# GpSimd's block-by-block weight copies, later output weights and a ScalarE read-out in a convolution and gated feed-forward kernel

## The chip, the core and the metric

The kernel runs on one core of a Trainium2 chip. The metric is the device time in microseconds of one execution; lower is better. Three runs of the kernel before took 766.85, 766.41 and 765.5 us, with a median of 766.41 us. A profiled execution of the same kernel took 766.03 us; its trace covers a span of 764.2 us of that.

The core's engines work side by side, each through its own list of instructions in order: TensorE (PE for its matmuls, PEld for the loads of its stationary operand), VectorE (DVE), ScalarE (ACT), GpSimd (POOL) and SyncE (SP), which here only issues DMA requests. They wait for one another through semaphores.

## The reference

The input x has 8 sequences of 4096 tokens with 192 values. First comes a causal convolution with 7 taps, whose taps are a softmax over the rows of `weight`, one row for each of 8 heads of 24 channels. Its output goes through a gated feed-forward layer.

```python
w = softmax(weight)                      # [8 heads, 7 taps]
x_pad = concatenate([zeros(6 tokens), x])
c[t, h, :] = sum_k w[h, k] * x_pad[t + k, h, :]
gate = maximum(c @ w_gate, 0)            # 192 -> 1536
val  = c @ w_val                         # 192 -> 1536
out  = (gate * val) @ w_out              # 1536 -> 192
```

Activations and weights are float16 in the kernel, sums are float32, and the output is float32.

## The kernel before

**Units and blocks.** Tokens are worked on in 16 units (`NUNIT`). A unit holds 1024 tokens of each of two sequences, called streams: one lies on partitions 0 to 63, the other on 64 to 127. The 192 channels are three chunks `c` of 64. For each unit `gate_val` (line 526) runs twice, once for each window `w` of 512 tokens. A run goes through 12 blocks `f` of 128 hidden columns. A block does six matmuls with `Wg` (three chunks, two streams) and six with `Wv` (line 539), into two PSUM tiles; ScalarE applies the ReLU to the first (line 550) and VectorE multiplies with the second into `hT` (line 551). So block `f` of the first window needs columns 128f to 128f+127 of `Wg` and `Wv`, on both halves of the partitions. After both windows `project` (line 634) multiplies `hT` with `Wo` (line 568), and the results are copied out of PSUM and stored.

**PSUM.** There are four tiles of two banks, used in turn, so a block's tile is free again when its reader of two blocks earlier has finished.

**Where the convolved tokens come from.** For unit 0 the convolution itself runs on TensorE as products with banded matrices (`conv_dense`, line 344). `first_block` (line 371) does the first window before anything else: one PSUM tile for each chunk, copied to `xc[0]` by ScalarE for chunks 0 and 1 and by VectorE for chunk 2 (line 379). `second_block` does the second window in front of block 5 (line 530). From unit 1 on, ScalarE, VectorE and GpSimd convolve from a transposed copy of x, the "lane". `lane_load(v)` (line 187) requests x for unit v into `x_e`, in two pieces with two streams each. `lane_turn(v)` (line 456) is a generator: for each piece GpSimd copies both streams from `x_e` into `x_p` (line 463), then SyncE requests DMA transposes of its tiles into `x_r` (line 467), and then it yields. `load_x(2)` requests a last group of tokens for TensorE's convolution, for the part of unit 1 that the lane does not cover; the steps "x" and "y" of the first projection use it.

**The weights at the start.** `load_w(s)` (line 158) requests slice `s` of `Wg` and of `Wv` from GpSimd's queue, for partitions 0 to 63 alone. The slices are cut at columns 0, 128, 384, 640, 896, 1152 and 1536: slice 0 is block 0, slice 1 blocks 1 and 2, slice 2 blocks 3 and 4, slice 3 blocks 5 and 6, slice 4 blocks 7 and 8, slice 5 blocks 9 to 11. The other half of the partitions is then filled by copies. VectorE makes those of slices 0 (in `first_block`) and 1 (line 692). GpSimd makes those of slices 2 to 5: `pool_halves` copies a slice of `Wg`, then of `Wv`, with one instruction each, and `pool_parts` (slice 2) splits that of `Wv` by blocks.

**The order on GpSimd's queue.** Requests and copies are worked off in the order in which the code names them; a request waits for GpSimd to reach it. After the requests of slices 0 to 2 come two of `load_x(1)`, those of slice 3, the copies of slice 2, the requests of slice 4, `Wg`'s of slice 5, the copies of slice 3, and `Wv`'s request of slice 5 (lines 217 to 226). Lines 694 to 702 go on: the copies of slice 4, the request of `Wo`, the copies of slice 5, the four requests of `lane_load(1)`, the copy of the taps to the upper partitions, two requests of `load_x(2)`, four small memsets in the band tiles, and `lane_turn(1)` with its four copies.

Of the kernel before, what the change touches and what calls it, by code (L numbers as in the profile page):

```python
# [16 lines left out]
def kernel(  # L17
# [12 lines left out]
    nc = tc.nc  # L30
# [7 lines left out]
    NCH = D // 64  # L38
    NBLK = D // 32
    NFF = DFF // 128  # L40
    WIN = 512
# [48 lines left out]
    def load_rest(steps):  # L90
        for _ in steps:
            pass
# [11 lines left out]
    def stage(p0, rows, st, n_st, jj, n):  # L104
        at = room[p0 : p0 + rows, 0, 0, 0:1]
        dims = [[D * GSUB, n_st], [D, n], [1, D]]
        return bass.AP(
            tensor=at.tensor,
            offset=at.offset + D * (GSUB * st + jj),
            ap=[at.ap[0]] + [d for d in dims if d[1] > 1],  # L110
        )
# [3 lines left out]
    def body(st):  # L115
# [11 lines left out]
        out=xts[0][PAD : PAD + FIRST, 0, :, :],  # L127
        in_=bass.AP(
            tensor=x.tensor, offset=x.offset, ap=[[D, FIRST], [NB * S * D, 2], [1, D]]
        ),  # L130
# [22 lines left out]
    Wg = const.tile([128, NCH, DFF], F16)  # L153
    Wv = const.tile([128, NCH, DFF], F16)
    Wo = const.tile([128, NFF, D], F16)
    CUTS = [0, 128, 384, 640, 896, 1152, DFF]

    def load_w(s, which=3):
        cols = slice(CUTS[s], CUTS[s + 1])
        for src, dst in ((moe_w_gate, Wg), (moe_w_val, Wv))[which == 2 : 1 + (which > 1)]:  # L160
            nc.gpsimd.dma_start(
                out=dst[0:64, :, cols],
                in_=src.rearrange("(c p) f -> p c f", p=64)[:, :, cols],
            )

    def both_halves(copy, s, dst):
        cols = slice(CUTS[s], CUTS[s + 1])
        copy(out=dst[64:128, :, cols], in_=dst[0:64, :, cols])

    def pool_halves(s):  # L170
        both_halves(nc.gpsimd.tensor_copy, s, Wg)
        both_halves(nc.gpsimd.tensor_copy, s, Wv)

    def pool_parts(s):
        both_halves(nc.gpsimd.tensor_copy, s, Wg)
        for f0 in range(CUTS[s], CUTS[s + 1], 128):
            nc.gpsimd.tensor_copy(out=Wv[64:128, :, f0 : f0 + 128], in_=Wv[0:64, :, f0 : f0 + 128])  # L177

    xes, xrs, accs, prods = {}, {}, {}, {}

    def pieces(v):
        both = [(0, TDVE, v * UNIT)]
        if v + 1 < NUNIT:
            both.append((TDVE, TILES - TDVE, (v + 1) * UNIT + LDVE))
        return both

    def lane_load(v, hold=None):


        xe = epool.tile([128, TILES, 2, NCH, 64], F16, name="x_e")  # L190
        xes[v] = xe
        for j0, n, t in pieces(v):
            bp, t0 = t // S, t % S
            start = int(t0 == 0)
            if start:
                nc.gpsimd.memset(xe[0:HALO, j0, :, :, :], 0.0)
            for st in range(2):
                b = bp + NB * st
                first = nc.gpsimd.dma_start(  # L199
                    out=xe[:, j0 + start : j0 + n, st, :, :].rearrange("p j c r -> p j (c r)"),  # L200
                    in_=bass.AP(
                        tensor=x.tensor,
                        offset=x.offset + (b * S + t0 - HALO + 128 * start) * D,
                        ap=[[D, 128], [128 * D, n - start], [1, D]],
                    ),
                )
                if hold is not None:
                    tc.add_manual_dep(first.ins, hold.ins.name, SYNC, reason="behind the turns of the lane before")
                    hold = None
                if start:  # L210
                    nc.gpsimd.dma_start(
                        out=xe[HALO:128, j0, st, :, :].rearrange("p c r -> p (c r)"),
                        in_=x[b, 0 : 128 - HALO, :],
                    )
                yield
# [3 lines left out]
    load_w(2)  # L219
    load_rest(load_x(1))  # L220
    load_w(3)
    pool_parts(2)
    load_w(4)
    load_w(5, 1)
    pool_halves(3)
    load_w(5, 2)

    ex = const.tile([H, KW + 1], FP)
    nc.vector.memset(ex[:, KW : KW + 1], 1e-9)
# [21 lines left out]
    with nc.allow_low_precision("zero and one"):  # L251
        nc.vector.tensor_tensor(
            out=same[:], in0=col[:, 0:SEG], in1=s_of[:].to_broadcast([SUB, SEG]), op=ALU.is_equal
        )
        nc.vector.tensor_scalar(
            out=places[:, SUB - SEG : SUB - SEG + NROW],
# [7 lines left out]
        out=mx[:], in_=wr[:], axis=mybir.AxisListType.X, op=ALU.max, negate=True  # L264
# [6 lines left out]
    with nc.allow_low_precision("rounded as the band is"):  # L271
        nc.vector.tensor_scalar(
            out=soft[:],
# [7 lines left out]
        out=spread[0:SUB, 0, 0:H],  # L281
# [7 lines left out]
    with nc.allow_low_precision("products with one and zero"):  # L289
        nc.vector.tensor_tensor(  # L290
            out=diag[:],
# [6 lines left out]
    for a in range(2):  # L298
        for b in range(NSEG):
            nc.tensor.matmul(  # L300
                out=(bps, spread)[a][:, a, HB * SEG * b : HB * SEG * (b + 1)],
# [9 lines left out]
    for cols in (slice(0, 64), slice(64, D)):  # L311
        nc.scalar.copy(
            out=xts[0][0:ROWS0, 1:GSUB, 0, cols],
            in_=stage(0, ROWS0, 0, 1, 1, GSUB - 1)[:, :, cols],
# [25 lines left out]
    xc = {}  # L340
# [30 lines left out]
    def first_block():  # L371
        xc[0] = xcpool.tile([128, NCH, UNIT], F16, name="xc")
        both_halves(nc.vector.tensor_copy, 0, Wg)
        both_halves(nc.vector.tensor_copy, 0, Wv)
        for c in range(NCH):
            ps = psum.tile([128, 2, 512], FP, name="ps")
            conv_dense(0, c, ps, 0)
            copy = nc.vector.tensor_copy if c == 2 else nc.scalar.copy
            copy(out=xc[0][:, c, 0:WIN], in_=ps[:, 0, :])

    def second_block():
        two, one = [psum.tile([128, 2, 512], FP, name="ps") for _ in range(2)]
        conv_dense(1, 0, two, 0)
        conv_dense(1, 1, two, 1)
        nc.scalar.copy(out=xc[0][:, 0:2, WIN : 2 * WIN], in_=two[:])
        conv_dense(1, 2, one, 0)
        nc.vector.tensor_copy(out=xc[0][:, 2, WIN : 2 * WIN], in_=one[:, 0, :])
# [68 lines left out]
    def lane_turn(v):  # L456
        xe = xes.pop(v)
        xp = epool.tile([128, TILES, NCH, 2, 64], F16, name="x_p")
        xr = rpool.tile([128, NCH, 128 * TILES], F16, name="x_r")
        xrs[v] = xr  # L460
        for j0, n, _ in pieces(v):
            for st in range(2):
                nc.gpsimd.tensor_copy(  # L463
                    out=xp[:, j0 : j0 + n, :, st, :], in_=xe[:, j0 : j0 + n, st, :, :]
                )
            for j in range(j0, j0 + n):
                nc.sync.dma_start_transpose(
                    out=xr[:, :, 128 * j : 128 * j + 128],
                    in_=xp[:, j].rearrange("p c s r -> p (c s r)"),
                )  # L470
            yield
# [54 lines left out]
    def gate_val(u, w):  # L526
        h = hpool.tile([128, NFF, 2, WIN], F16, name="hT")
        xcb = xc[u]
        for f in range(NFF):
            if u == 0 and w == 0 and f == 5:  # L530
                second_block()
            pss = [psum.tile([128, 2, 512], FP, name="ps") for _ in range(2)]
            order = [(i, c) for i in range(2) for c in range(NCH)]
            if u == 0 and w == 0 and f == 0:
                order = [(i, c) for c in range(NCH) for i in range(2)]
            for i, c in order:
                W = (Wg, Wv)[i]
                for st in range(2):
                    nc.tensor.matmul(  # L539
                        out=pss[i][:, st, :],  # L540
                        lhsT=W[64 * st : 64 * st + 64, c, 128 * f : 128 * (f + 1)],
                        rhs=xcb[64 * st : 64 * st + 64, c, WIN * w : WIN * (w + 1)],
                        start=(c == 0),
                        stop=(c == NCH - 1),
                        tile_position=(64 * st, 0),
                    )
            by_stream = u == 0 and w == 0 and f < 2
            for sts in (slice(0, 1), slice(1, 2)) if by_stream else (slice(0, 2),):
                gr = gpool.tile([128, 2, WIN], F16, name="gr")
                nc.scalar.activation(out=gr[:, sts], in_=pss[0][:, sts], func=ACTF.Relu)  # L550
                nc.vector.tensor_tensor(  # L551
                    out=h[:, f, sts], in0=gr[:, sts], in1=pss[1][:, sts], op=ALU.mult
                )
        return h
# [127 lines left out]
    for h in range(H):  # L682
        r = G * h
        while r < G * (h + 1):
            c, n = r // 64, min(64 - r % 64, G * (h + 1) - r)
            nc.sync.dma_start(
                out=tap[r % 64 : r % 64 + n, c, :],
                in_=taps[h : h + 1, :].unsqueeze(1).to_broadcast([1, n, KW]),
# [2 lines left out]

    both_halves(nc.vector.tensor_copy, 1, Wg)
    both_halves(nc.vector.tensor_copy, 1, Wv)
    pool_halves(4)
    nc.gpsimd.dma_start(out=Wo[:], in_=moe_w_out.rearrange("(c p) d -> p c d", p=128))
    pool_halves(5)
    load_rest(lane_load(1))
    nc.gpsimd.tensor_copy(out=tap[64:128], in_=tap[0:64])
    load_rest(load_x(2))
    for end in ends:  # L700
        nc.gpsimd.memset(end, 0.0)
    load_rest(lane_turn(1))
    for u in range(NUNIT):
        adds = 1 <= u < NUNIT - 1
        if u + 1 < NUNIT:
# [63 lines left out]
```

## Time and profile before

| | |
|---|---|
| median of 3 runs | 766.41 us (765.5 to 766.85) |
| the profiled execution's own time | 766.03 us |
| its span | 764.2 us |
| HBM read, written | 31.48 MB, 25.17 MB |
| DMA packets of GpSimd's queue (q0) | 41104, 20.6% of 16 engines' span |
| DMA packets of SyncE's and ScalarE's queue (q1) | 90472, 23.3% |

The profile page gives for each engine the time in which it was busy, a chain of waits followed back from the last instruction, and groups of instructions by line with the engine's idle time ahead of them. A row of the timeline reads: start in us from the span's begin, duration, engine, line, operation, output tile and input tiles, shape, count, and in brackets the idle time of the engine ahead of it with what ended that. "POOL L161 DMA_DIRECT2D" is the time in which GpSimd makes a request; the transfer itself goes on behind it. A row of the DMA view gives for requests of one kind their count, the size, and the median time from the start of the request to the landing of its data; a row without a last number has a landing that could not be told. The rows of the queues give packets, megabytes and the share of 16 DMA engines in the view's window.

### The profile page before, as it was taken

What the parts mean: (1) busy time and instruction counts of PE and PEld (TensorE: products, weight loads), DVE (VectorE), ACT (ScalarE), POOL (GpSimd) and SP (SyncE); (2) the same over time, 40 slices, a digit from 0 to 9 for tenths busy, and PEclk for the clock granted to TensorE, in tenths of its full rate; (3) what the DMA queues carried; (4) which work ended last, traced back from release to release, by engine and by line L of the source; (5) the groups of instructions that cost most, each with busy time, mean ns of one, the idle gap of its engine ahead of it and who ended that gap; (6) DMA issues with size and microseconds to landing.
All of it is one profiled execution on the core that took longest, in us unless ns stands there. A gap on an engine that the chain in (4) does not pass through costs nothing.

```text
span 764.2 us, 25118 instructions
## 1 busy us (share of the span) xinstructions
PE 760.4 (99%) x10935; PEld 518.6 (68%) x10935; DVE 705.7 (92%) x768; ACT 600.3 (79%) x733; POOL 378.8 (50%) x249
## 2 busy tenths in 40 slices
PE   9999999999999999999999999999999999999998
PEld 4495775957659576585866858567595775957658
DVE  7998999999999999999999999999999999999891
ACT  6787887878878787887878878787887887876571
POOL 8519448093571916629175390853909347090000
PEclk9999999999999999999999999999999999999999
DMA  9969037280442805529162281832818034220202
GB/s 117 130 111 145 7 97 79 65 114 22 95 64 84 95 24 109 46 85 95 32 113 36 85 94 44 107 29 90 88 44 130 8 98 60 64 49 16 70 1 84
DMA packets 131830, 55.93 MB, mean 73 GB/s; under 512 B 96584, under 2 KB 131720, under 8 KB 131720
## 3 DMA queue, kind: packets, MB, share of 16 engines
q1 hardware_dynamic: 90472, 38.66, 23.3%
q0 software_dynamic: 41104, 15.57, 20.6%
q8 instruction: 85, 1.39, 0.8%
q14 instruction: 25, 0.20, 0.1%
q10 hardware_dynamic: 144, 0.10, 0.0%
HBM read 31.48 MB, written 25.17 MB: 74 GB/s over the span
## 4 chain that ended last, share of the span: by engine, by line
PE 99%; ACT 0%; issue 0%
PE ps L539 65%; PE ps L568 32%; PE ps L617 1%; PE ps L145 0%; PE ps L361 0%; PE ps L300 0%; PE ps L402 0%; ACT acc L594 0%; PE ps L280 0%
## 5 line engine op out<-in xcount | busy, mean ns | idle before, releaser
L551 DVE TENSOR_TENSOR hT<-gr,ps 128x1024 f16<-128x1024 f16 (+1 forms) x386 | 469.1, 1216 | 36.2 <-ACT gr L550 9.4
L550 ACT ACTIVATE gr<-ps 128x1024 f16<-128x1024 f32 (+1 forms) x386 | 393.3, 1020 | 102.5 <-PE ps L539 100.6
L489 POOL TENSOR_TENSOR prods<-prods 128x1344 f32<-128x1344 f32 x70 | 212.3, 3032 | 289.8 <-DVE prods L485 286.4
L539 PE MATMUL ps<-xc,Wv 64*128 64x512 f16 x2304 | 316.6, 376 | 0.0
L539 PE MATMUL ps<-xc,Wg 64*128 64x512 f16 x2304 | 316.2, 376 | 0.0
L568 PE MATMUL ps<-Wo,hT 64*128 64x192 f16 x5952 | 248.8, 243 | 0.0
L568 PEld LDWEIGHTS <-hT 64*128 64x128 f16 x5952 | 246.4, 94 | 3.5
L539 PEld LDWEIGHTS <-Wv 64*128 64x128 f16 x2304 | 136.0, 94 | 113.4 <-POOL Wv L177 0.4
L539 PEld LDWEIGHTS <-Wg 64*128 64x128 f16 x2304 | 123.7, 94 | 121.4 <-issue 0.4
L513 DVE SCALAR_TENSOR_TENSOR acc<-x_r,tap,acc 128x576 f32<-128x576 f16 x225 | 165.3, 811 | 0.0
L483 ACT ACTIVATE prods<-x_r,tap 128x448 f32<-128x448 f16 x222 | 130.0, 660 | 0.0
L594 ACT COPY out_s<-ps 128x768 f32<-128x768 f32 (+1 forms) x64 | 45.6, 713 | 51.2 <-PE ps L568 39.8
L199 POOL DMA_DIRECT2D x_e<-in_x_dram x58 | 47.0, 822 | 15.3 <-ACT acc L499 11.5
L463 POOL COPY x_p<-x_e 128x960 f16<-128x960 f16 (+1 forms) x58 | 50.3, 907 | 0.7 <-DMA x_e<-in_x_dram 0.7
L489 POOL TENSOR_TENSOR xc<-prods 128x1344 f16<-128x1344 f32 x14 | 42.4, 3030 | 1.1
L513 DVE SCALAR_TENSOR_TENSOR xc<-x_r,tap,acc 128x576 f16<-128x576 f16 x45 | 34.1, 811 | 0.0
L499 ACT ACTIVATE acc<-x_r,tap 128x576 f32<-128x576 f16 x45 | 31.4, 763 | 0.0
L485 DVE TENSOR_SCALAR prods<-x_r,tap 128x448 f32<-128x448 f16 x70 | 26.6, 448 | 0.0
L594 DVE COPY out_s<-ps 128x384 f32<-128x384 f32 (+1 forms) x16 | 8.6, 540 | 11.5 <-PE ps L617 9.4
L617 PE MATMUL ps<-Wo,hT 128*128 128x192 f16 x96 | 8.1, 246 | 0.0
L617 PEld LDWEIGHTS <-hT 128*128 128x128 f16 x96 | 7.9, 98 | 0.2 <-issue 0.2
L145 PE MATMUL ps<-const-bfloat16-1.0 128*128 128x512 bf16 (+1 forms) x8 | 3.8, 609 | 0.8 <-PEq L753 0.8
(56 smaller groups left out, 55.9 us busy)
## 6 DMA issues: line engine op xcount, KB each, us to landing
out_dram<-out_s SPq DMA_DIRECT2D x62, 384.0 KB, 2.7
x_e<-in_x_dram POOLq DMA_DIRECT2D x34, 192.0 KB, 7.5
x_e<-in_x_dram POOLq DMA_DIRECT2D x24, 240.0 KB, 5.0
x_r<-x_p SPq DMA_TRANSPOSE x131, 4.7
Wo<-in_moe_w_out_dram POOLq DMA_DIRECT2D x1, 576.0 KB, 6.6
x_h<-in_x_dram POOLq DMA_DIRECT2D x2, 210.0 KB, 6.1
Wg<-in_moe_w_gate_dram POOLq DMA_DIRECT2D x4, 96.0 KB, 4.8
Wv<-in_moe_w_val_dram POOLq DMA_DIRECT2D x4, 96.0 KB, 5.8
```

Of the source, the lines that this page charges most:

```text
L199: first = nc.gpsimd.dma_start(out=xe[:, j0 + start : j0 + n, st, :, :].rearrange("p j c r -> p j (c r)"), in_=bass.AP(tensor=x.tensor, off ...
L463: nc.gpsimd.tensor_copy(out=xp[:, j0 : j0 + n, :, st, :], in_=xe[:, j0 : j0 + n, st, :, :])
L483: engine.activation(out=out, in_=in_, func=ACTF.Copy, scale=scale)
L485: engine.tensor_scalar(out=out, in0=in_, scalar1=scale, scalar2=None, op0=ALU.mult)
L489: nc.gpsimd.tensor_tensor(out=pr[:, 0] if k < KW - 1 else xc[v + 1][:, :, LDVE:UNIT], in0=pr[:, 0], in1=pr[:, k], op=ALU.add,)
L499: nc.scalar.activation(out=accs[v][:, c, :], in_=shifted(v, c, 0, 0), func=ACTF.Copy, scale=tap[:, c, 0:1],)
L513: nc.vector.scalar_tensor_tensor(out=xc[v][:, c, 0:LDVE] if k == KW - 1 else acc[:, c, :], in0=shifted(v, c, k, 0), scalar=tap[:, c, k : k ...
L539: nc.tensor.matmul(out=pss[i][:, st, :], lhsT=W[64 * st : 64 * st + 64, c, 128 * f : 128 * (f + 1)], rhs=xcb[64 * st : 64 * st + 64, c, WI ...
L550: nc.scalar.activation(out=gr[:, sts], in_=pss[0][:, sts], func=ACTF.Relu)
L551: nc.vector.tensor_tensor(out=h[:, f, sts], in0=gr[:, sts], in1=pss[1][:, sts], op=ALU.mult)
L568: mm = nc.tensor.matmul(out=outs[q], lhsT=h[64 * r : 64 * r + 64, f, st, 128 * q : 128 * (q + 1)], rhs=Wo[64 * r : 64 * r + 64, f, :], sta ...
L594: one(out=dst[:, step * j : step * j + step], in_=src[:, step * j : step * j + step])
```

## The change

GpSimd's copies of slices 3, 4 and 5 are made block by block, `Wg` and `Wv` in turn, by `pool_blocks`; each becomes an instruction with 128 columns in three chunks, where it had 256 or 384. Both requests of slice 5 stand together behind the copies of blocks 5 and 6. The requests of `lane_load(1)` come right behind the copies of block 11, then the first half of `lane_turn(1)`, and only then the request of `Wo`. The tap copy, `load_x(2)` and the memsets follow as before, and the second half of `lane_turn(1)` stands at the end. Slice 2 is copied as before (the same three instructions, written out in place). ScalarE now reads out all three chunks of the first convolution. In the very first block TensorE does both first chunks of `Wg`, then both of `Wv`, then the third of each, where it took the chunks in turn.

```diff
-    def load_w(s, which=3):
+    def load_w(s):
         cols = slice(CUTS[s], CUTS[s + 1])
-        for src, dst in ((moe_w_gate, Wg), (moe_w_val, Wv))[which == 2 : 1 + (which > 1)]:
+        for src, dst in ((moe_w_gate, Wg), (moe_w_val, Wv)):
...
-    def pool_halves(s):
-        both_halves(nc.gpsimd.tensor_copy, s, Wg)
-        both_halves(nc.gpsimd.tensor_copy, s, Wv)
-
-    def pool_parts(s):
-        both_halves(nc.gpsimd.tensor_copy, s, Wg)
-        for f0 in range(CUTS[s], CUTS[s + 1], 128):
-            nc.gpsimd.tensor_copy(out=Wv[64:128, :, f0 : f0 + 128], in_=Wv[0:64, :, f0 : f0 + 128])
+    def pool_blocks(*blocks):
+        for f in blocks:
+            cols = slice(128 * f, 128 * f + 128)
+            for dst in (Wg, Wv):
+                nc.gpsimd.tensor_copy(out=dst[64:128, :, cols], in_=dst[0:64, :, cols])
...
     load_w(2)
     load_rest(load_x(1))
     load_w(3)
-    pool_parts(2)
+    both_halves(nc.gpsimd.tensor_copy, 2, Wg)
+    for f in (3, 4):
+        cols = slice(128 * f, 128 * f + 128)
+        nc.gpsimd.tensor_copy(out=Wv[64:128, :, cols], in_=Wv[0:64, :, cols])
     load_w(4)
-    load_w(5, 1)
-    pool_halves(3)
-    load_w(5, 2)
+    pool_blocks(5, 6)
+    load_w(5)
...
             conv_dense(0, c, ps, 0)
-            copy = nc.vector.tensor_copy if c == 2 else nc.scalar.copy
-            copy(out=xc[0][:, c, 0:WIN], in_=ps[:, 0, :])
+            nc.scalar.copy(out=xc[0][:, c, 0:WIN], in_=ps[:, 0, :])
...
             if u == 0 and w == 0 and f == 0:
-                order = [(i, c) for c in range(NCH) for i in range(2)]
+                order = [(0, 0), (0, 1), (1, 0), (1, 1), (0, 2), (1, 2)]
...
     both_halves(nc.vector.tensor_copy, 1, Wg)
     both_halves(nc.vector.tensor_copy, 1, Wv)
-    pool_halves(4)
+    pool_blocks(7, 8, 9, 10, 11)
+    load_rest(lane_load(1))
+    turns = lane_turn(1)
+    next(turns)
     nc.gpsimd.dma_start(out=Wo[:], in_=moe_w_out.rearrange("(c p) d -> p c d", p=128))
-    pool_halves(5)
-    load_rest(lane_load(1))
     nc.gpsimd.tensor_copy(out=tap[64:128], in_=tap[0:64])
     load_rest(load_x(2))
     for end in ends:
         nc.gpsimd.memset(end, 0.0)
-    load_rest(lane_turn(1))
+    load_rest(turns)
```

## The prediction

> **What bounds the kernel now.** I read the page first, for the engine that the end hangs on.
>
> ```profile
> span 764.2 us, 25118 instructions
> PE 760.4 (99%) x10935; PEld 518.6 (68%) x10935; DVE 705.7 (92%) x768; ACT 600.3 (79%) x733; POOL 378.8 (50%) x249
> ...
> PE 99%; ACT 0%; issue 0%
> ```
>
> TensorE fills the span and nearly the whole chain of waits. A change that takes no matmul away can only pay where TensorE stands still, and the edits touch work of the first 50 us. So the second view is TensorE's timeline there (start, length, engine, line, operation).
>
> ```profile
> 7.16 0.39 PE L539 MATMUL ps<-xc,Wg 64*128 64x512 f16 x2
> ...
> 8.33 0.39 PE L539 MATMUL ps<-xc,Wg 64*128 64x512 f16 x2
> ...
> 8.76 0.84 PE L539 MATMUL ps<-xc,Wg 64*128 64x512 f16 x6
> ...
> 11.39 0.81 PE L539 MATMUL ps<-xc,Wg 64*128 64x512 f16 x6
> ...
> 12.88 1.02 PE L539 MATMUL ps<-xc,Wg 64*128 64x512 f16 x6
> ...
> 14.48 1.55 PE L361 MATMUL ps<-band,x_h 110*32 110x104 f16 x120
> 15.96 0.82 PE L539 MATMUL ps<-xc,Wg 64*128 64x512 f16 x6
> ...
> 21.16 0.81 PE L539 MATMUL ps<-xc,Wg 64*128 64x512 f16 x6
> 21.80 0.81 PE L539 MATMUL ps<-xc,Wv 64*128 64x512 f16 x6
> ```
>
> Blocks 5 and 9 begin at 15.96 and 21.16, so a block takes 5.20/4 = 1.30 us and each half of it 0.65: TensorE's own pace. Blocks 0 to 4, from 7.16 to the second convolution at 14.48, take 7.32 us where five blocks at that pace are 6.50. All standing still in the head is thus 0.82 us, and no repair of the head can gain more.
>
> The last place in it where TensorE waits is block 3, which begins at 11.39 and should give way to block 4 at 12.69 but does at 12.88. Two rows name the reason, and the DMA view gives the landing.
>
> ```profile
> 6.06 0.63 POOL L161 DMA_DIRECT2D Wv<-in_moe_w_val_dram  x1
> ...
> 11.88 0.95 POOL L177 COPY Wv<-Wv 64x384 f16<-64x384 f16 x2 [1.45 <-DMA Wv<-in_moe_w_val_dram]
> ...
> 12.43 0.33 PEld L539 LDWEIGHTS <-Wv 64*128 64x128 f16 x5 [0.36 <-POOL Wv L177]
> ...
> Wv<-in_moe_w_val_dram POOLq DMA_DIRECT2D x1, 96.0 KB, 5.8
> ```
>
> Slice 2 of Wv is requested at 6.06, lands 5.8 us later at 11.86, GpSimd copies it from 11.88, and TensorE goes on at 12.43. From there to the second convolution and beyond, every start keeps its pace. So block 3's Wv is a gate: what TensorE gains ahead of it is lost there, unless the gate itself moves.
>
> **The change part by part.** *ScalarE's read-out and the new order in block 0.*
>
> ```profile
> 6.36 1.07 ACT L379 CAST xc<-ps 128x512 f16<-128x512 f32 x2 [0.65 <-PE ps L361]
> ...
> 7.11 0.45 DVE L168 COPY Wv<-Wv 64x384 f16<-64x384 f16 x1 [0.27 <-DMA Wv<-in_moe_w_val_dram]
> ...
> 7.59 0.69 DVE L379 CAST xc<-ps 128x512 f16<-128x512 f32 x1
> ```
>
> VectorE begins chunk 2 only when its Wv copy is over (7.56), ends at 8.28, and TensorE takes chunk 2 at 8.33. ScalarE's two copies fill 1.07, with starts 0.48 apart, so a third runs from about 7.33 to 7.92 and chunk 2 is ready 0.36 us earlier. The new order needs chunk 1 (7.43) second and Wv third, which lands and is copied by 7.56. At 0.216 for a pair of matmuls (0.65/3): first chunk 7.16, Wg's second 7.49, Wv's two 7.70 and 7.92, the third chunk 8.14 and 8.35, block 1 at 8.57. That is 0.19 us ahead of the 8.76 of now. VectorE, rid of 0.69 us, must still wait for slice 1 to land, which I bound between 7.56 and its present copy at 8.31; either way it is not later than now. On the taps' side ScalarE is 0.5 us later, and with it ten small requests on SyncE's queue whose data are needed only at 40 us.
>
> All of this lies ahead of the gate. The requests up to slice 3 and the copies of slice 2 stay in their order on GpSimd's queue, and nothing that VectorE gives up delays them. I take Wv's landing at 11.86 again: the 0.19 us turn into a longer wait at block 3. **0.0 us**; if the gate opened early enough, at most 0.19 (lead) + 0.19 (the gate's own loss) = −0.38.
>
> *Copies by block.* The costs come from GpSimd's timeline.
>
> ```profile
> 8.93 0.64 POOL L161 DMA_DIRECT2D Wv<-in_moe_w_val_dram  x1
> ...
> 14.65 0.84 POOL L168 COPY Wg<-Wg 64x768 f16<-64x768 f16 x1
> ...
> 16.18 0.63 POOL L161 DMA_DIRECT2D Wv<-in_moe_w_val_dram  x1
> ...
> 18.34 1.08 POOL L695 DMA_DIRECT2D Wo<-in_moe_w_out_dram  x1
> 19.42 1.16 POOL L168 COPY Wg<-Wg 64x1152 f16<-64x1152 f16 x1
> ...
> 21.60 3.22 POOL L199 DMA_DIRECT2D x_e<-in_x_dram  x4
> ...
> 26.66 1.90 POOL L463 COPY x_p<-x_e 128x960 f16<-128x960 f16 x2
> ...
> Wv<-in_moe_w_val_dram POOLq DMA_DIRECT2D x1, 96.0 KB, 5.7
> Wg<-in_moe_w_gate_dram POOLq DMA_DIRECT2D x1, 144.0 KB, 3.8
> Wv<-in_moe_w_val_dram POOLq DMA_DIRECT2D x1, 144.0 KB, 3.0
> ```
>
> Starts are 0.45 apart for a copy of one block (two fill 0.95, with an overlap of 0.05), (16.18−14.65)/2 = 0.765 for two blocks, (21.60−19.42)/2 = 1.09 for three. An instruction so costs about 0.14 us beside 0.315 a block. Slices 3 and 4 gain two instructions each and slice 5 four: 8 × 0.14 = 1.1 us more on GpSimd. The Wo request that leaves this stretch takes 1.08 away. The two cancel, and what counts is each block's deadline.
>
> Slice 3's Wv lands at 8.93+5.7 = 14.63. Block 5's Wg copy runs by then; 5 Wv, 6 Wg, 6 Wv start at 14.65, 15.10, 15.55, and the requests of slice 5 at 16.0 and 16.63. Blocks 7 and 8 start at 17.26, 17.71, 18.16, 18.61. Slice 5 lands after 3.0 to 3.8 us: Wg between 19.0 and 19.8, Wv between 19.6 and 20.4. So block 9's copies end by 20.3 and 20.9, and TensorE takes them at 21.16 and 21.80: 0.9 us to spare, where now the slice's Wv copy ends at 21.66, 0.14 ahead. Blocks 10 and 11 follow at 0.45 a copy against TensorE's 0.65. **0.0 us**; bounds below. A gain is excluded here, as no row of TensorE after 12.43 names a weight copy.
>
> *x first, Wo behind it.* The last copy starts 2.25 us after block 9's Wg at the earliest (19.06) and 1.8 after its Wv at the latest (20.4), so the x_e requests begin between 21.8 and 22.65 (now 21.60). The rest of the chain:
>
> ```profile
> 28.59 13.05 SPq L467 DMA_TRANSPOSE x_r<-x_p  x9
> ...
> 40.58 2.14 PE L568 MATMUL ps<-Wo,hT 64*128 64x192 f16 x48
> ...
> 43.06 2.89 ACT L483 ACTIVATE prods<-x_r,tap 128x448 f32<-128x448 f16 x5
> ...
> 47.22 0.80 ACT L594 COPY out_s<-ps 128x768 f32<-128x768 f32 x1 [0.54 <-PE ps L568]
> ...
> x_e<-in_x_dram POOLq DMA_DIRECT2D x2, 240.0 KB, 4.8
> Wo<-in_moe_w_out_dram POOLq DMA_DIRECT2D x1, 576.0 KB, 6.6
> x_r<-x_p SPq DMA_TRANSPOSE x2, 2.5
> ```
>
> GpSimd now waits for x_e ahead of Wo, and behind that wait stand Wo, the tap copy, two x_h requests, the memsets and the second piece. The second stream's request begins 0.87 after the first and lands 4.8 later, at 27.5 to 28.3; its copy takes 0.95, so Wo is requested at 28.4 to 29.3 and lands 6.6 later, at 35.0 to 35.9. TensorE takes it at 40.58: 4.7 us to spare. The two x_h, a third of Wo's bytes each, are requested by 31.2 and, even at Wo's 6.6, land by 37; TensorE takes them after the first half projection, at 42.7. The second piece's copies end by 34.1, and SyncE reaches its transposes only after five others (5/9 of 13.05 us from 28.4 on: 35.7), so they are not late by it. The nine transposes as a whole shift by −0.2 to +0.7. The last lands now at 28.59+13.05−1.26+2.5 = 42.9, and ScalarE's products that read it start at 43.06, so these can start up to 0.5 late. ScalarE has 0.54 us idle ahead of 47.22, and the bank that this copy frees is wanted after 40.58 + four half projections of 2.15, beyond 49. **0.0 us**.
>
> The sum is 0.0 against the profiled execution's 766.03 us. Its runs gave a median of 766.41, 0.38 higher, so I put the time at 766.3.
>
> **The rivals.** *Wo comes late (slower).* It decides when Wo lands after 40.58. For it: Wo's request now sits behind a wait for x, and its transfer meets the transposes of 28.59 to 41.64, which the old one, over by 24.9, did not. If sharing doubles Wo's 6.6 us to 13.2 from 29.3 on, it lands at 42.5, TensorE stands 1.9 us: 768.3. Against it: it must take 11.3 us, and the two kinds already overlapped for the last x_e and x_h. The Trainium skill (DMA: Bandwidth & Descriptors, section SWDGE vs HWDGE vs iDMA) says that requests of GpSimd and of SyncE feed different queues inside a DMA engine, which serves them in turn; by that the doubling would be the worst case, and no row of this trace shows Wo beside transposes.
>
> *Block 9 waits.* Slice 5's Wv is requested at 16.63 instead of 16.18. At the 5.8 us of the slowest row it lands at 22.4, its copy ends at 22.95, and TensorE stands 1.2 us at 21.80: 767.6. Against it: that row came from the crowded first 12 us; both rows of slice 5 are under 4.
>
> *The gate opens earlier.* A queue's row bears on it, of the stretch from 8.2 to 10.5 us.
>
> ```profile
> q8 instruction: 1, 0.02, 5.8%
> ```
>
> One packet of instructions took 5.8% of 16 engines over 2.3 us, which is 2.1 us of one engine, just while Wv's slice 2 was on its way. If it is what made 5.8 us of that landing, a shift of it against Wv would open the gate: −0.38, or 766.0; with every stall of the head gone −0.82, or 765.6. The Trainium skill (Runtime: NRT & Kernel Launch, section Instruction fetch mechanics) says that an engine's instructions come by DMA in blocks of 16 KiB, asked for by its own sequencer as it runs; the packet's 0.02 MB agrees. Against the rival: the first convolution, before which nothing changes, has brought TensorE through its first 240 instructions already, and the requests before slice 3 keep their times.
>
> *The change doesn't do what it says* can be left out for the copies; for the read-out it is the gate again.
>
> **How the numbers follow.** About 0.2% (1.53 us) is what a measurement of this kernel can tell from no change. No net effect beyond 0.4 us: 0.75. Gate opening: 0.10, within 0.2% since its most is 0.82. Block 9: 0.06, also within it. Wo late: 0.05, slower. Left over, 0.02 each for faster and slower by something not seen. So faster 0.02, same 0.91, slower 0.07. The single runs spread from 765.5 to 766.85; the range goes from 765.2 (the gate's 0.38 and half of that spread, 0.7) to 767.6 (block 9's price).
>
> **What would show it.** Right: ScalarE's row of line 379 counts three, TensorE's block 1 starts near 8.57, the weight load of block 3's Wv still waits for GpSimd to about 12.43, block 4 starts near 12.88 and the convolution at 14.48; Wo's first matmul at 40.6, with its request near 29. Wrong: a gap in TensorE's rows at block 9 or ahead of Wo's first matmul, or Wv's copy of slice 2 starting clearly before 11.8.

## The result, and the profile after

The changed kernel takes 768.13 us (median of 17 runs, 767.32 to 770.86) against 766.07 for the kernel before (17 runs, 765.5 to 769.6): 2.06 us more, a ratio of 1.0026 with a 95% interval of [1.0017, 1.0035]. The forecast was no difference, with a range that ended at 767.6.

The profiled execution of the changed kernel took 767.42 us, 1.39 more than the one of before; its span is 1.1 us longer. From its page, the head line and the chain of waits:

```profile
span 765.3 us, 25127 instructions
...
PE 97%; DMA 2%; POOL 0%; issue 0%; ACT 0%; POOLq 0%
```

The chain was all TensorE before. Now 2% of it is a DMA, and the line below it in the page gives x_h as its target. Where time is lost is read from TensorE's own starts. The head first (timeline, columns as before):

```profile
8.59 0.86 PE L537 MATMUL ps<-xc,Wg 64*128 64x512 f16 x6
...
12.52 0.81 PE L537 MATMUL ps<-xc,Wg 64*128 64x512 f16 x6
...
13.91 1.59 PE L360 MATMUL ps<-band,x_h 110*32 110x104 f16 x120
15.43 0.82 PE L537 MATMUL ps<-xc,Wg 64*128 64x512 f16 x6
```

Block 1 starts at 8.59 as worked out (8.57). Block 4 starts at 12.52 and block 5 at 15.43, where they started at 12.88 and 15.96: in this execution the gate at block 3 opened early, and TensorE was 0.53 us ahead. Then the first projection and unit 1:

```profile
10.90 0.96 POOL L222 COPY Wv<-Wv 64x384 f16<-64x384 f16 x2 [0.46 <-DMA Wv<-in_moe_w_val_dram]
...
22.01 3.26 POOL L196 DMA_DIRECT2D x_e<-in_x_dram  x4
...
28.60 0.98 POOL L461 COPY x_p<-x_e 128x960 f16<-128x960 f16 x1 [1.48 <-DMA x_e<-in_x_dram]
29.53 1.03 POOL L696 DMA_DIRECT2D Wo<-in_moe_w_out_dram  x1
...
40.45 2.15 PE L566 MATMUL ps<-Wo,hT 64*128 64x192 f16 x48 [0.21 <-DMA Wo<-in_moe_w_out_dram]
43.50 0.34 PE L400 MATMUL ps<-x_h,band 64*128 64x192 f16 x4 [0.90 <-DMA x_h<-in_x_dram]
...
43.78 2.11 ACT L497 ACTIVATE acc<-x_r,tap 128x576 f32<-128x576 f16 x3 [3.13 <-DMA x_r<-x_p]
...
59.32 0.84 PE L537 MATMUL ps<-xc,Wg 64*128 64x512 f16 x6
...
60.14 0.82 PE L537 MATMUL ps<-xc,Wv 64*128 64x512 f16 x6
```

- Wo's first matmul should come at 40.58 − 0.53 = 40.05 and comes at 40.45: 0.40 lost.
- The half projection ahead of x_h's matmuls took 40.58 to 42.56 before, so these should start at 42.43. They start at 43.50: 1.07 lost.
- In unit 1 the second Wv group starts 0.82 after its Wg group instead of 0.65. The profile names no releaser for it. VectorE's last read-out of the projection ends at 60.09, 0.05 ahead of that start, so I read it as a wait for VectorE, whose sums had begun 2.69 us late behind ScalarE's first sum (line 497), which waited 3.13 us for the transposed x: 0.17 lost.

So −0.53 + 0.40 + 1.07 + 0.17 = 1.1, the span's difference. From there to the end TensorE's starts keep this distance. The DMA view of the requests of 29 to 36 us shows the cause next to hand; its last row is of the kernel before, for the transposes requested from 28 to 34 us:

```profile
Wo<-in_moe_w_out_dram POOLq DMA_DIRECT2D x1, 576.0 KB, 10.9
x_h<-in_x_dram POOLq DMA_DIRECT2D x2, 192.0 KB, 11.9
x_r<-x_p SPq DMA_TRANSPOSE x4, 7.4
...
x_r<-x_p SPq DMA_TRANSPOSE x4, 4.1
```

Wo lands after 10.9 us (6.6 before), x_h after 11.9, and the first transposes after 7.4 (4.1 before). Those requested from 37 to 41 us land after 6.2, where the last ones of before took 2.5.

### The profile page after: what moved, and what is told of

It reads as the page before. It is cut to its first block, busy times and chain, and to the rows that moved or that the text cites. A ratio compares the mean times of both kernels' runs of the same rounds, so it can differ in the third digit from the quotient of the medians.

```text
span 765.3 us, 25127 instructions
## 1 busy us (share of the span) xinstructions
PE 760.0 (99%) x10935; PEld 526.4 (69%) x10935; DVE 705.1 (92%) x767; ACT 600.8 (78%) x734; POOL 380.0 (50%) x257
## 3 DMA queue, kind: packets, MB, share of 16 engines
q8 instruction: 85, 1.39, 0.8%
## 4 chain that ended last, share of the span: by engine, by line
PE 97%; DMA 2%; POOL 0%; issue 0%; ACT 0%; POOLq 0%
PE ps L537 64%; PE ps L566 32%; DMA x_h<-in_x_dram 2%; PE ps L615 1%; PE ps L360 0%; POOL x_h L125 0%; PE ps L400 0%; POOL x_h L87 0%; ACT acc L592 0%; POOL tap L697 0%; POOL steps L124 0%; POOLq L124 0%; POOLq L752 0%
## 5 line engine op out<-in xcount | busy, mean ns | idle before, releaser
L537 PEld LDWEIGHTS <-Wv 64*128 64x128 f16 x2304 | 138.2, 94 | 110.4 <-issue 0.6
L537 PEld LDWEIGHTS <-Wg 64*128 64x128 f16 x2304 | 129.1, 94 | 115.9 <-issue 0.2
## 6 DMA issues: line engine op xcount, KB each, us to landing
Wo<-in_moe_w_out_dram POOLq DMA_DIRECT2D x1, 576.0 KB, 10.9
```

The costliest lines, as they stand in the source:

```text
L537: nc.tensor.matmul(out=pss[i][:, st, :], lhsT=W[64 * st : 64 * st + 64, c, 128 * f : 128 * (f + 1)], rhs=xcb[64 * st : 64 * st + 64, c, WI ...
```

## The experiments

From this trace I held theory T: the moved requests of Wo and x_h run beside the transposes and both sides are slowed. Its rivals put the loss on the copies by block, whose eight instructions make x late (R1, later L), or on the head's edits (H). Each kernel below was run in five rounds with the kernel before on the same chip. They form four series: the first four kernels, the next four, the next four, and the last three. In the last three series the kernel before itself had a few executions of 770 to 774 us, which makes the intervals there wide, so medians are compared first. Its median was 765.93 in the first and second series, 766.07 in the third and 766.04 in the fourth.

**The move undone, the rest of the change kept.**

```diff
-    pool_blocks(7, 8, 9, 10, 11)
+    pool_blocks(7, 8)
+    (request of Wo)
+    pool_blocks(9, 10, 11)
     load_rest(lane_load(1))
-    turns = lane_turn(1); next(turns); (request of Wo)
...
-    load_rest(turns)
+    load_rest(lane_turn(1))
```

> The changed kernel with the move of Wo alone undone: Wo is requested between the copies of blocks 8 and 9, and both halves of lane_turn(1) stand at the end again. Theory T (collision: Wo and x_h are late because their transfers now run beside the transposes): Wo's first matmul and the x_h matmuls wait for no DMA, the head's gain of about 0.5 us stays, so 0.3 to 0.6 us below the kernel before (ratio about 0.9994) and about 2 us below the changed kernel. Rival R1 (the copies by block, eight instructions more, make the loss, because x and the transposes behind them come later): about 1 to 1.6 us above the kernel before, as in the changed kernel. Rival R2 (ScalarE's and VectorE's lateness in the first projection makes the loss): as R1, since the transposes begin no earlier here.

Measured: 767.63 us (12 runs), ratio 1.003 [1.0015, 1.0045]. T missed: with the move gone, a loss of 1.7 us stays. In the timeline Wo and x_h wait for nothing, but ScalarE does, and then TensorE for ScalarE:

```profile
45.92 2.90 ACT L481 ACTIVATE prods<-x_r,tap 128x448 f32<-128x448 f16 x5 [3.28 <-DMA x_r<-x_p]
...
49.61 8.10 PE L566 MATMUL ps<-Wo,hT 64*128 64x192 f16 x192 [0.78 <-ACT y L425]
```

ScalarE's products wait 3.28 us for the second piece of the transposed x. The read-outs behind them in its queue are late, and TensorE waits for the bank.

**Wo alone back in its place.**

```diff
-    pool_blocks(7, 8, 9, 10, 11)
+    pool_blocks(7, 8)
+    (request of Wo)
+    pool_blocks(9, 10, 11)
     load_rest(lane_load(1))
     turns = lane_turn(1)
     next(turns)
-    (request of Wo)
```

> The changed kernel with Wo requested between the copies of blocks 8 and 9, while the first half of lane_turn(1) stays ahead of load_x(2). Theory T: Wo waits for nothing; x_h, requested near 30 to 31, shares the DMA engines with the transposes alone and lands after 7 to 9 us, by 40, ahead of 42.1; so 0.3 to 0.6 us below the kernel before. If x_h alone is enough for the collision: its matmuls start up to 1 us late, and the time is 0.5 us above the kernel before. R1: 1 us or more above.

Measured: 768.03 us, ratio 1.0037 [1.002, 1.0054]. T had it below the kernel before, and it is 2.1 us above. The profiled execution says little: its first convolution was slow (118 matmuls took 2.75 us, 1.67 in the profile of the next experiment), TensorE was 1.65 us behind from block 0 on, and with that delay nothing waited later.

**x_h ahead of the wait, Wo behind it.**

```diff
     load_rest(lane_load(1))
+    load_rest(load_x(2))
     turns = lane_turn(1)
```

> The changed kernel with load_x(2) requested right behind lane_load(1), ahead of the first half of lane_turn(1); Wo stays behind it. Theory T: x_h lands by 34, so its wait of 0.9 us is gone; Wo still lands near 40, its matmul 0.2 to 0.4 us late; the time is within 0.3 us of the kernel before, some 1.5 us below the changed kernel. If Wo alone carries the loss: as the changed kernel, 1.4 us or more above the kernel before. R1: as the changed kernel.

Measured: 767.81 us, ratio 1.0019 [1.0007, 1.003]. TensorE's wait for x_h is gone and that for Wo stays, as T had it, but the time is 1.9 us above the kernel before instead of within 0.3: the gain was used up by ScalarE's lateness.

```profile
41.16 2.15 PE L566 MATMUL ps<-Wo,hT 64*128 64x192 f16 x48 [0.53 <-DMA Wo<-in_moe_w_out_dram]
...
47.15 2.91 ACT L481 ACTIVATE prods<-x_r,tap 128x448 f32<-128x448 f16 x5 [2.91 <-DMA x_r<-x_p]
...
50.84 8.10 PE L566 MATMUL ps<-Wo,hT 64*128 64x192 f16 x192 [0.91 <-ACT y L425]
```

**The move alone, on the kernel before** (whole copies; the diff is that of the first experiment turned round, with `pool_halves`).

> The kernel before with the move alone: the copies of slices 3 to 5 stay whole, Wo goes behind lane_load(1) and the first half of lane_turn(1). x is requested about 1.1 us earlier than before, near 20.5, and Wo near 27.5 to 28. Theory T with the landing times of the changed kernel (10.9 us for Wo, 11.9 for x_h): Wo lands near 38.7, x_h near 41.5, both just in time; between 0 and 0.5 us above the kernel before. Rival R3 (the move costs by itself, wherever the copies end): 1.5 us or more above. R1: no loss.

Measured: 766.77 us (11 runs), ratio 1.0006 [0.9997, 1.0014]; 0.84 above the kernel before, which the interval does not tell from none. x is requested at 19.77, Wo at 27.55, and neither Wo nor x_h is waited for, as expected. But x's transposes are held up beside them, although x was requested early: ScalarE's first sum waited 1.72 us and its products 1.60, and TensorE 0.94 for ScalarE. So T holds for the transposes, and is not the whole.

**The copies by block alone, on the kernel before.**

```diff
     load_w(4)
-    load_w(5, 1); pool_halves(3); load_w(5, 2)
+    pool_blocks(5, 6)
+    load_w(5)
...
-    pool_halves(4)
+    pool_blocks(7, 8)
     (request of Wo)
-    pool_halves(5)
+    pool_blocks(9, 10, 11)
```

> The kernel before with the copies by block alone, both requests of slice 5 behind the copies of blocks 5 and 6, Wo between the copies of blocks 8 and 9; no move, read-out and order of block 0 as before. Theory L (x is late: GpSimd's eight more instructions push the x_e requests from 21.6 to about 22.4, the transposes begin 0.8 to 1.8 us later, ScalarE's products wait 1 to 3 us for them in the first projection, and TensorE then waits for a bank that ScalarE frees): 0.6 to 1.8 us above the kernel before. Theory T (collision through the move alone): no difference. Rival H (ScalarE's read-out and the new order in block 0 make the loss): no difference.

Measured: 771.53 us (766.91 to 775.29), ratio 1.0061 [1.0033, 1.0089]: 5.6 us more, the largest loss of any part, and three times the most that L had expected. The chain in its timeline, and the landing of the last transpose:

```profile
22.90 3.22 POOL L205 DMA_DIRECT2D x_e<-in_x_dram  x4
...
42.00 3.19 POOL L205 DMA_DIRECT2D x_e<-in_x_dram  x4 [9.26 <-ACT acc L504]
...
48.75 2.90 ACT L488 ACTIVATE prods<-x_r,tap 128x448 f32<-128x448 f16 x5 [5.97 <-DMA x_r<-x_p]
...
52.44 3.80 PE L573 MATMUL ps<-Wo,hT 64*128 64x192 f16 x53 [3.33 <-ACT y L432]
...
x_r<-x_p SPq DMA_TRANSPOSE x1, 6.7
```

x is requested 1.3 us later than before (21.60); the products start 5.7 us later (43.06). The second row names the amplifier: `lane_load(2)`, unit 2's x, is let go at 42.0 by ScalarE's first sum, which needs only the first piece of unit 1's x. The last transpose of the second piece is still under way and lands after 6.7 us instead of 2.5. (In the kernel before, `lane_load(2)` went at 42.38, when the last transpose had some 0.5 us to go.)

A second price comes on top, and it is not the DMA's. The granted clock is the share of its full clock that TensorE is given. In this profile TensorE stood still for 3.33 us up to 52.44, and the clock then was 0.50 from 52 to 55 us and 0.80 from 55 to 56. The 192 matmuls that follow the wait took 9.51 us, where the same 192 took 8.10 in the first experiment, whose wait was 0.78 us and whose clock stayed at 1.00. So the wait's 3.3 us and the clock's 1.4 make up the 4.7 us by which this span is longer than that of the kernel before. The runs show the same: 11 of the 12 have a mean granted clock of 0.996 to 0.998 and take 770 us or more; the one at 1.000 takes 766.91.

**The head alone, on the kernel before.**

```diff
-            copy = nc.vector.tensor_copy if c == 2 else nc.scalar.copy
-            copy(out=xc[0][:, c, 0:WIN], in_=ps[:, 0, :])
+            nc.scalar.copy(out=xc[0][:, c, 0:WIN], in_=ps[:, 0, :])
...
-                order = [(i, c) for c in range(NCH) for i in range(2)]
+                order = [(0, 0), (0, 1), (1, 0), (1, 1), (0, 2), (1, 2)]
```

> The kernel before with ScalarE's read-out of the third chunk and the new order of block 0 alone. Theory L: x is not later, so between 0.5 us below and 0.2 above the kernel before (what the head gains is lost where ScalarE's products wait for x). Rival H: 1 us or more above. The gate at block 3 tells besides whether its opening at 10.9 goes with these edits or differs between executions.

Measured: 766.25 us, ratio 0.9991 [0.9969, 1.0013]. No gain and no loss that can be told: H falls.

**A delay alone, on the kernel before.**

```diff
     pool_halves(5)
+    idle = const.tile([128, NCH, 256], F16)
+    nc.gpsimd.tensor_copy(out=idle[64:128], in_=Wg[0:64, :, 640:896])
     load_rest(lane_load(1))
```

> The kernel before with one more copy on GpSimd ahead of lane_load(1), of two blocks of Wg into a tile that nobody reads: 0.77 us of delay and nothing else. Theory L: the x_e requests begin at 22.4, ScalarE's products wait for x, and the time is 0.3 to 1.5 us above the kernel before. Theories T and H: no difference.

Measured: 767.90 us, ratio 1.0018 [0.9991, 1.0046]. Six of its twelve runs lie at 765.7 to 766.8, six at 769.0 to 771.4. Above 769 us lay two of the 35 runs of the kernel before beside them. The copy, which nobody reads, makes x 0.97 us later in the profile; it costs 2 us in the median and 3 to 5.5 us in the long six, four of which have a mean granted clock of 0.998. The profiled execution (766.69 us) was one of the mild ones, and even there:

```profile
22.57 3.22 POOL L199 DMA_DIRECT2D x_e<-in_x_dram  x4
...
46.14 2.91 ACT L483 ACTIVATE prods<-x_r,tap 128x448 f32<-128x448 f16 x5 [2.63 <-DMA x_r<-x_p]
```

So a delay alone brings L's wait and its loss. L had the size wrong: 2.0 us in the median against 0.3 to 1.5, and in two groups.

**The head, and Wo right behind the x_e requests (ahead of every wait), whole copies.**

```diff
-    (request of Wo)
     pool_halves(5)
     load_rest(lane_load(1))
+    (request of Wo)
     nc.gpsimd.tensor_copy(out=tap[64:128], in_=tap[0:64])
```

> The kernel before with the read-out and order of block 0, whole copies, and Wo requested right behind the four x_e requests, ahead of the tap copy and of every wait for x. Theory L: x is requested 1.1 us earlier, near 20.5, Wo lands near 31, the transposes begin by 28 and ScalarE waits for nothing; 0.2 to 0.6 us below the kernel before. If Wo's transfer, now between x and x_h, delays x_h or the transposes: no gain, or up to 0.5 us above.

Measured: 765.97 us (765.79 to 767.7), ratio 0.9991 [0.9969, 1.0013]. In the profile ScalarE waited for no x (x was requested at 20.33), but the expected 0.2 to 0.6 us did not show: an earlier x only keeps the loss away.

**The amplifier taken from the copies by block.** `lane_load(2)` is held by ScalarE's first product, which reads the second piece, instead of its first sum.

```diff
             for c, k in work[i]:
-                product(nc.scalar, u + 1, c, k)
+            made = [product(nc.scalar, u + 1, c, k) for c, k in work[i]]
+            if u == 0 and i == 0:
+                load_rest(lane_load(2, made[0]))
...
-                load_rest(lane_load(2, begun))
```

> The copies by block alone (as in the run with 771.53 us), with one more edit: the requests of lane_load(2) wait for ScalarE's first product instead of its first sum of the first projection. Theory C (x's late transposes run into the requests of lane_load(2), which ScalarE's first sum lets go at 42.0 although five more tiles are still to land; that collision turns 0.8 us into 6): the last transposes land about 2.5 us after their request at 41.9, the products begin near 44.4, and the time is 0 to 1.2 us above the kernel before. Rival D (the transposes themselves are slow once they start late, or x_h and Wo hold them up): products at 47 or later, 4 us or more above.

Measured: 766.65 us (765.63 to 767.82), ratio 0.9997 [0.9973, 1.0022]. The same copies that cost 5.6 us cost 0.6. From its timeline, and the DMA view from 42.5 to 44.5 us and from 41.9 to 42.3:

```profile
45.97 2.91 ACT L488 ACTIVATE prods<-x_r,tap 128x448 f32<-128x448 f16 x5 [2.97 <-DMA x_r<-x_p]
...
47.19 3.19 POOL L205 DMA_DIRECT2D x_e<-in_x_dram  x4 [14.76 <-ACT prods L488]
...
q8 instruction: 1, 0.02, 5.0%
...
x_r<-x_p SPq DMA_TRANSPOSE x1, 4.0
```

The products were expected at 44.4 and came at 45.97: the last transpose landed after 4.0 us, not 2.5. In that stretch an instruction packet took 5.0% of 16 engines over 2 us, 1.6 us of one engine, as much as the miss. That this packet is the cause of it was not tried by itself.

**The same hold on the changed kernel** (diff as above).

> The changed kernel with lane_load(2) waiting for ScalarE's first product. In its profile lane_load(2) was requested at 45.45, later than the last transpose, because ScalarE's first sum itself waited to 43.78. Theory T+C (in the changed kernel Wo and x_h carry the loss, beside the transposes): Wo's and x_h's waits stay, 1.2 to 2.2 us above the kernel before. If lane_load(2) carries it here too: 0 to 0.8 us above.

Measured: 768.21 us, ratio 1.0014 [0.9989, 1.0038]; unchanged, as T and C had it together. In its timeline x_h's and the sum's waits are those of the changed kernel:

```profile
43.52 0.34 PE L400 MATMUL ps<-x_h,band 64*128 64x192 f16 x4 [1.04 <-DMA x_h<-in_x_dram]
...
43.79 2.11 ACT L497 ACTIVATE acc<-x_r,tap 128x576 f32<-128x576 f16 x3 [2.95 <-DMA x_r<-x_p]
```

**All requests ahead of the waits in the changed kernel, with the hold and without.**

```diff
     load_rest(lane_load(1))
+    (request of Wo)
+    load_rest(load_x(2))
     turns = lane_turn(1)
     next(turns)
-    (request of Wo)
     nc.gpsimd.tensor_copy(out=tap[64:128], in_=tap[0:64])
-    load_rest(load_x(2))
```

> The changed kernel with Wo and load_x(2) requested right behind lane_load(1), ahead of every wait for x, and lane_load(2) waiting for the first product. Theory T+C: Wo and x_h land by 35, no transfer runs beside the last transposes, products begin by 44.5: 0 to 0.8 us above the kernel before. If lateness alone costs: 1 us or more above.

> The same without the later lane_load(2). Theory T+C: Wo and x_h wait for nothing, but ScalarE's first sum runs on time, lets lane_load(2) go near 42, and the last transposes land late as in the runs with the copies by block: products near 46 or later, 1 to 5 us above the kernel before, and clearly above the version with the later lane_load(2).

Measured: 766.65 us with the later `lane_load(2)` (ratio 0.9989 [0.9963, 1.0014]), 767.82 without (766.1 to 772.23; 1.002 [0.9997, 1.0043]). Both lie within what T and C had together, though the products came at 45.82 with it, not by 44.5. The profiled execution without it, one of the long ones at 772.23 us, shows how far the collision goes:

```profile
49.91 2.90 ACT L481 ACTIVATE prods<-x_r,tap 128x448 f32<-128x448 f16 x5 [7.19 <-DMA x_r<-x_p]
...
53.60 8.64 PE L566 MATMUL ps<-Wo,hT 64*128 64x192 f16 x169 [4.03 <-ACT y L425]
```

Here too the granted clock fell behind TensorE's wait of 4.03 us: it was 0.62 from 53 to 54 us, 0.50 to 56 and 0.67 to 57.

So two edits of order, one for each collision, take 1.5 of the changed kernel's 2.06 us back; each alone leaves it 2.1 and 1.75 us above the kernel before (768.21 and 767.82).

**The hold alone on the kernel before, and two tries for a faster kernel** (Wo right behind the x_e requests and the hold, without and with the head's edits).

> The kernel before with lane_load(2) waiting for ScalarE's first product, and nothing else. Theory C says that the kernel before stands at the edge itself (its last transpose lands 0.2 us ahead of its reader, and some of its runs take 770 to 774 us): the same median within 0.3 us, and no run above 768. Rival (the later lane_load(2) costs by itself, which would be the 0.6 us left in the two versions with it): 0.4 us or more above the kernel before.

> The kernel before with Wo requested behind the four x_e requests (x 1.1 us earlier) and lane_load(2) waiting for the first product; no copies by block, read-out and order as before. Theory C: last transposes land by 42, ScalarE waits for nothing, the median is 0 to 0.4 us below the kernel before, and no run is above 767.5.

> The same with ScalarE's read-out and the changed order of block 0. If these gain anything once x is in time: 0.2 us or more below the version without them. If the gate at block 3 (slice 2 of Wv and an instruction packet) decides the head in every execution: equal to it within 0.2 us.

Measured: 766.01 us (0.999 [0.9969, 1.001]), 766.03 us (0.9996 [0.9976, 1.0016]) and 765.97 us (0.9993 [0.9974, 1.0012]). None differs from the kernel before's 766.04 by more than 0.07 us in the median; the forecast of no run above 767.5 for the second missed by little (767.65). The hold costs nothing that can be told, so I put the 0.6 us left above down to x's lateness that remains.

The hold also seems to take the long executions away. Over all series 13 of 151 runs of the kernel before lie above 769 us, and none of the 36 of these three, whose longest is 767.97. Chance alone could do that, but the granted clock says more: it is 0.996 to 0.998 in each of the 12 of these 13 for which it is on record, and 0.999 or more in each of the 72 runs of the six kernels with the hold. The profile of the hold alone (766.80 us) shows the case: x's first stream landed late by itself, its copy waiting 1.84 us, so the products started at 46.21 instead of 43.06, and TensorE's longest wait was 0.71 us. No long execution of the kernel before was profiled, so that these had the same collision is argued, not shown.

## Why the prediction was wrong, step by step

*The bound.* Right: TensorE's pace rules, and all of the loss lies in the first 61 us.

*The head.* Block 1 came at 8.59 as worked out, and the conclusion that the head's edits alone bring nothing held (766.25 against 765.93). But the lead of 0.19 us belonged to one execution. Block 0 took 1.60 us in the profile of before, where VectorE's Wv copy had waited for its data (the row at 7.11); in the six other profiles with the old head it took 1.31, and with the new one 1.37 in eight of ten (in the other two the first convolution was slow already). So the new order gains nothing even there. What failed besides is "I take Wv's landing at 11.86 again": in the changed kernel the copy began at 10.90. But it began about as early (10.53, 10.68) in the two kernels with the copies or the move alone, which keep the old head, and late again (12.08) in the kernel with the delay alone. So the gate differs between executions and not by the edit, and so does the 0.53 us of the changed kernel's profile: its second convolution starts at 13.91, and those of these two kernels with the old head at 13.91 and 13.89. The rows for the instruction packet, 8.2 to 10.5 us, first of the changed kernel and then of the delay, next to 5.8% in the kernel before:

```profile
q8 instruction: 1, 0.02, 2.4%
```

```profile
q8 instruction: 1, 0.02, 7.2%
```

That is 0.9 us of one DMA engine where the gate opened at 10.9, and 2.1 and 2.6 us where it opened at 11.9 and 12.1. The section Instruction fetch mechanics of the Trainium skill's page Runtime: NRT & Kernel Launch, on blocks of 16 KiB by DMA, agrees with the 0.02 MB; it calls the cost mostly hidden, and here a slow packet goes along with about 1 us at the gate. That the packet is the cause is not shown. In the last kernel a packet of 1.9 us went with a copy at 12.01, but in the one with x_h first a packet of 1.8 us, begun later, at 9.08, left the gate open at 10.37.

*Copies by block.* The durations were right, 0.45 us a copy, x requested at 22.0 within the forecast 21.8 to 22.65, and block 9 never waited. The step that failed is "the two cancel, and what counts is each block's deadline". The deadline that counted was x's. Alone, these copies cost 5.6 us, and a bare delay of their kind 2.0; in the one profile that splits it, 1.4 of 4.7 us were TensorE's lower clock behind its wait, which the prediction did not have either.

*x first, Wo behind it.* This is the part that lost the time in the changed kernel. Two terms were mis-sized. Wo's landing was taken at 6.6 us from a time without transposes and was 10.9; x_h's at 6.6 and was 11.9. That is the rival "Wo comes late", which I gave 0.05 and priced for Wo alone, while x_h lost more (1.07 against 0.40); that its 768.3 lies near the measured 768.13 is luck. A third was a little short: the second stream's x landed after 5.6 us instead of 4.8, so Wo's request came at 29.53, behind the forecast 28.4 to 29.3, and the transposes began 1.02 us later, not 0.7 at most. And "these can start up to 0.5 late. ScalarE has 0.54 us idle ahead of 47.22" took the transposes' landing times over from the kernel before and left out ScalarE's first sum, which waited 3.13 us. The landing times are not constants: beside Wo and x_h they were 7.4 and 6.2 us, beside `lane_load(2)` 6.7. I had the number that should have warned me, a last landing 0.2 us ahead of its reader, and asked only whether a small shift would fit, not what the transposes would run into when they came later. What stood next was `lane_load(2)`, let go at a time that does not move with them.

*The parts together.* They do not add: 5.6 (copies), 0.8 (move) and 0.3 (head, not told from none) against 2.06 for all. In the changed kernel's profile the first sum itself waits for x to 43.78, so `lane_load(2)` is requested only at 45.45, after the last transpose has been issued. The move takes the copies' collision away and puts its own in place.

## What to carry to other kernels

When a margin is a few tenths of a microsecond, ask what the late transfer would collide with, not only whether its reader has slack: here about 1 us of delay cost 2 us in the median and up to 5.5. Look at the granted clock behind a long wait as well: part of the price can be there. A landing time read from a trace holds for the traffic of that moment, so a moved request needs a price for its new company. Hold a prefetch behind a reader of the last transfer that it may disturb, not of the first; on the kernel before that was free in the median, and no long execution was seen with it.

## What the runs showed of the hardware

DMA requests of GpSimd and transposes requested by SyncE were both slower where they overlapped: Wo's landing went from 6.6 to 10.9 us, the first transposes' from 4.1 to 7.4, and a last transpose's from 2.5 to 6.7 beside `lane_load(2)`. The Trainium skill (DMA: Bandwidth & Descriptors, section SWDGE vs HWDGE vs iDMA) has the two kinds served in turn inside an engine; a doubling as the worst case held for Wo (1.7 times) and the first transposes (1.8 times) but not for the last one (2.7 times).

In the two profiles where TensorE stood still for 3.33 and 4.03 us its granted clock fell to 0.50; behind waits of up to 1.04 us it stayed at 1.00. How long a wait it takes was not tried.

A single 16 KiB packet of instructions took 0.9 to 2.6 us of one DMA engine in the head. I had not expected it to be long enough to be seen in a weight's landing, and three of the four slowest (1.8 to 2.6 us) went along with the three latest gates (11.88 to 12.08). That it causes them was not tried by itself.
